# Routing tables of an attention and MoE kernel in 16 bits with columns innermost, and the first expert's low parts behind the slots' description

## The chip, the cores and the metric

The kernel runs on one core of one Trainium2 chip. Its time is the device time of one execution in microseconds (us); the median of three runs is 889.3 us (888.17 to 893.38).

## The reference

Three layers follow one another. Attention with a forget gate runs over 4 batches, 8 heads, 576 positions and a head dimension of 64: the scores get `cum[i] - cum[j]` of the logarithm of the gates added, then a causal mask, a softmax and the product with v. Its output is x, 2304 tokens of 512. A mixture of experts follows: each token goes to the one of 8 experts whose logit is greatest.

```python
e_idx = np.argmax(x @ w_gate, axis=1)
for e in range(E):
    mask = e_idx == e
    h = np.maximum(x[mask] @ w1[e], 0.0)
    out[mask] = gate_w[mask, None] * eom[mask, e, None] * (h @ w2[e])
```

Here w1[e] is 512 x 1024 and w2[e] is 1024 x 512. A dense layer of width 2048 with a rational activation ends it. All results are float32; TensorE's operands are kept as a high and a low part, with three products each.

## The kernel before

**Attention.** 16 pairs of heads are worked through, and a planner (class Plan) orders their instructions from costs and due times; it writes the order of all engines, which is then fixed. For each pair GpSimd (POOL) makes three arrays for each of the two heads: kl (L416), the low half of qs (L425) and q2s (L430). TensorE's scores (L456 and L457) need them. Between these POOL sends six DMAs (L873) that fill with zeros the part of y_d that only a spill would write. Small constant arrays are made by POOL at the start (L928 to L936): s1 with the slot numbers, row with the 128 places of a slot, tokv with the tokens' numbers.

**Routing.** Tokens are sorted by expert into slots of 128 rows. For the 20 columns of 128 tokens, VectorE (DVE) finds each token's position `pos` (L1003), its slot `sidx` (L1007) and its place in the slot `pp` (L1009). From these it builds one-hot arrays: `so` (column x slot, L1012), `rs` (`so` times the token's number, L1015) and `op_` (column x place, L1021, four instructions for five columns each, as float32 against float32 into float16). TensorE multiplies `op_` and `rs` for all 20 columns into `pid` (L1026), and DVE converts that to integers: `ids` (L1028), the token in each place of each slot. Meanwhile x is scaled, and SP stores it to x_d (L823), five stores for the last batch.

**Slots.** POOL gathers the rows of x of slot s from x_d with an indirect DMA by `ids` (gather, L1203); three are sent at once. TensorE runs 24 matmuls without use in between (warm, L1347), then transposes slot 0 (trans_x, L1222), ScalarE (ACT) and DVE split it into colAh (L1097) and colAl (L1088), and the products with the expert's weights follow: mm1 (two halves of w1, units 0 and 1) and mm2 (two halves of w2, units 2 and 3). Each of these is four matmuls of the high parts (L1228), four with the low part of the slot's rows (L1235), four with the low part of the weights (L1231). split_unit makes the high part of a unit on ACT (L1056) and the low part on DVE (L1058), two instructions of 128 x 1024 each. slot_info (L1162 to L1185) is 21 small DVE instructions on 25 partitions; they write esl, from which SP, ACT, DVE and PE read whether a slot begins a new expert, and SP sends the next expert's weights (L1136) into `raw` once both parts of the unit there are made. The weights of the dense layer are decoded between the slots; the first decode's load is d8 (L1283) and its first DVE instruction is L1287.

Once the routing begins, the order on each engine is that of the program:

```python
for s in range(3):
    gather(s)
warm(24)
split_unit(0, hi=False)
split_unit(1, hi=False)
trans_x(0, col_of(0))
slot_info()
```

Of the kernel before, what the change touches and what calls it, by code (L numbers as in the profile page):

```python
# [9 lines left out]
F32 = mybir.dt.float32  # L10
F32R = mybir.dt.float32r
BF16 = mybir.dt.bfloat16
F16 = mybir.dt.float16
# [124 lines left out]
def tile_attention_moe_mlp(  # L138
# [81 lines left out]
    with ExitStack() as actx, ExitStack() as rctx:  # L220
# [646 lines left out]
        for u in range(4):  # L867
            plan.op((NPAIR - 5 + u) * SPAN, {"SP": 2900}, lambda e, u=u: nc.sync.dma_start(out=raw[u], in_=w_src(u, 0)), [st[NPAIR - 7 + u]["o_ot"]])
        n = 0
        for s in range(NPIPE, NSLOT):  # L870
            for c in range(0, DM, 2 * P):
                n += 1
                plan.op((2 + n // 2) * SPAN, {"POOL": 1100}, lambda e, s=s, c=c: nc.gpsimd.dma_start(  # L873
                    out=y_d[s * P : (s + 1) * P, c : c + 2 * P].rearrange("p (a q) -> p a q", q=P),
                    in_=qs[0].bitcast(F32)[:, :, S:],
                ), [st[2 + n // 2]["o_ot"]])
# [11 lines left out]
        with tc.manual_schedule():  # L888
            plan.emit()

# [37 lines left out]
        s1 = iota([P, NSLOT], [[1, NSLOT]], 0, 0, "s1")  # L928
        nc.gpsimd.tensor_scalar_add(s1, s1, ROUND)

        row = iota([P, P], [[-1, P]], 0, 0, "row")
        nc.gpsimd.tensor_scalar(row, row, 1.0 / P, (P - 1) / (2.0 * P), op0=ALU.mult, op1=ALU.add)
        pcol = iota([P, 1], [[0, 1]], 0, 1, "pcol", const)

        tokv = iota([P, B, NI], [[S, B], [P, NI]], -(NT // 2), 1, "tokv").rearrange("p b i -> p (b i)")
# [64 lines left out]
        for i in (3, 0, 4, 2, 1):  # L1000
# [7 lines left out]
        pp = t_([P, NCOL], name="pp")  # L1008
        nc.vector.scalar_tensor_tensor(pp, sidx, ROUND, pos, ALU.subtract, ALU.subtract)  # L1009
        SS = [P, NCOL, NSLOT]  # L1010
        so, rs = t_(SS, F16, name="so"), t_(SS, F16, name="rs")
        nc.vector.tensor_tensor(  # L1012
            so, s1.unsqueeze(1).to_broadcast(SS), sidx.unsqueeze(2).to_broadcast(SS), ALU.is_equal
        )
        nc.vector.tensor_tensor(rs, so, tokv.unsqueeze(2).to_broadcast(SS), ALU.mult)  # L1015
        op_ = ptp.tile([P, 2, NI, S], F32, tag="pT", name="op_").rearrange("p h i s -> p (h i s)").bitcast(F16)
        op_ = op_[:, : NCOL * P].rearrange("p (c q) -> p c q", q=P)
        pid = ps_r("pid")
        for c0 in range(0, NCOL, NI):
            cs = slice(c0, c0 + NI)  # L1020
            nc.vector.tensor_tensor(  # L1021
                op_[:, cs], row.unsqueeze(1).to_broadcast([P, NI, P]),
                pp[:, cs].unsqueeze(2).to_broadcast([P, NI, P]), ALU.is_equal,
            )
            for c in range(c0, c0 + NI):
# [35 lines left out]
    for u in range(4):  # L1061
        split_unit(u, lo=False)
# [588 lines left out]
```

## Time and profile before

| | us |
|---|---|
| median of three runs | 889.3 |
| the profiled execution | 889.93 |
| its span, from the first to the last instruction | 888.2 |
| what lies around the span | 1.7 |
| attention and routing, up to the write of `ids` | 211.4 |
| slots and the dense layer, from there to the end | 676.8 |

Times in the rows further down are counted from the start of the span. A row of a timeline has the start, the length, the engine, the line, the operation, the tiles written and read, their shape and type, the count of instructions merged, and in brackets the idle time of the engine just before and what ended it.

### The profile page before, as it was taken

The page shows a single profiled execution, that of the slowest core. Times are in us where ns is not written, and L with a number is a line of the kernel's source. Part 1 is how long each engine was busy: PE and PEld are TensorE (multiplying, and loading weights), DVE is VectorE, ACT ScalarE, POOL GpSimd, SP SyncE. Part 2 cuts the span into 40 slices and gives each one's busy share as a digit, 9 for nine tenths or more (in the row PEclk, how much of TensorE's full clock was granted, in tenths as well). Part 3 has the DMA queues.
Part 4 walks back from the last instruction along what each step waited for, and adds up shares of the span by engine and source line. Part 5 has one row for each costly group of instructions (what it writes and reads, how often), then busy time and mean ns, then how long its engine had stood idle before and what let it go on. Part 6 is the DMA issues. An engine that isn't in the chain of part 4 may idle for free. (4 is left out here: it accounts for less than half of the span.)

```text
span 888.2 us, 15292 instructions
## 1 busy us (share of the span) xinstructions
PE 849.3 (96%) x4667; PEld 705.0 (79%) x4667; DVE 747.9 (84%) x1428; ACT 615.6 (69%) x1282; POOL 337.5 (38%) x364
## 2 busy tenths in 40 slices
PE   6999898996999999999999999999999999999997
PEld 6787786764888887888787788899888889988885
DVE  7798999778798878778876999898898878988882
ACT  4889897876465667567545878777676667777772
POOL 7888586502113232223241233343233224324222
PEclk9999999997999999999999999999999999999999
DMA  6776567604866588789564121010000001000001
GB/s 167 167 182 168 154 175 212 199 27 151 298 218 217 177 263 310 226 288 316 195 218 154 48 72 37 0 60 24 13 36 25 12 1 57 16 1 36 1 0 48
DMA packets 49130, 110.32 MB, mean 124 GB/s; under 512 B 8405, under 2 KB 12526, under 8 KB 49038
## 3 DMA queue, kind: packets, MB, share of 16 engines
q1 hardware_dynamic: 36910, 69.90, 26.4%
q0 software_dynamic: 12128, 39.34, 13.3%
q8 instruction: 40, 0.66, 0.3%
q14 instruction: 52, 0.43, 0.2%
HBM read 151.79 MB, written 20.35 MB: 194 GB/s over the span
## 5 line engine op out<-in xcount | busy, mean ns | idle before, releaser
L1519 POOL TENSOR_TENSOR gl<-raw,gh 128x512 fp32r<-128x512 f32 (+1 forms) x71 | 84.2, 1186 | 207.3 <-ACT gh L1517 127.2
L1535 PE MATMUL pa<-wu,gl 128*128 128x512 f32 x256 | 100.6, 393 | 1.1 <-POOL gl L1519 1.1
L1533 PE MATMUL pa<-wu,gh 128*128 128x512 f32 x256 | 101.2, 395 | 0.0
L1534 PE MATMUL pa<-wu,gh 128*128 128x512 f32 x256 | 100.1, 391 | 0.0
L1492 ACT ACTIVATE raw<-ph 128x512 f32<-128x512 f32 (+1 forms) x80 | 44.3, 554 | 78.1 <-PE ph L1484 74.8
L1058 DVE TENSOR_TENSOR wu<-raw,wu 128x1024 fp32r<-128x1024 f32 x64 | 75.2, 1219 | 8.0 <-ACT wu L1056 6.6
L511 ACT ACTIVATE pr<-t,mn 128x384 f32<-128x384 f32 (+3 forms) x128 | 70.7, 557 | 16.0 <-DVE mn L479 15.4
L1505 DVE SCALAR_TENSOR_TENSOR raw<-raw,coef,raw 128x512 f32<-128x512 f32 (+1 forms) x80 | 66.2, 827 | 17.8 <-ACT raw L1501 15.1
L1495 DVE SCALAR_TENSOR_TENSOR raw<-raw,babs 128x512 f32<-128x512 f32 (+1 forms) x80 | 58.3, 729 | 20.9 <-ACT raw L1493 20.2
L1482 PE MATMUL ph<-colAh,wi 128*128 128x512 f32 x192 | 74.9, 390 | 1.0 <-ACTq L1423 0.7
L1484 PE MATMUL ph<-colAh,wi 128*128 128x512 f32 x192 | 74.7, 389 | 0.0
L1483 PE MATMUL ph<-colAl,wi 128*128 128x512 f32 x192 | 74.7, 389 | 0.0
L1056 ACT ACTIVATE wu<-raw 128x1024 fp32r<-128x1024 f32 x64 | 63.8, 1066 | 4.1 <-DMA raw<-in_w_dram 2.2
L479 DVE CUSTOM_DVE_ANT_0 t<-s,mask 128x384 f32<-128x384 f32 (+3 forms) x128 | 57.8, 484 | 6.5 <-PE s L457 3.0
L1506 DVE SCALAR_TENSOR_TENSOR raw<-raw,cbias 128x512 f32<-128x512 f32 (+1 forms) x80 | 57.6, 720 | 2.3
L1500 ACT ACTIVATE raw<-raw,cbias 128x512 f32<-128x512 f32 (+1 forms) x80 | 55.0, 687 | 6.3 <-DVE raw L1495 5.8
L1494 ACT ACTIVATE raw<-ph,neg 128x512 f32<-128x512 f32 (+1 forms) x80 | 59.3, 741 | 0.0
L1535 PEld LDWEIGHTS pa<-wu,gl 128*128 128x128 f32 x256 | 48.0, 188 | 12.7 <-POOL gl L1519 2.4
L1497 DVE SCALAR_TENSOR_TENSOR raw<-raw,coef,ph 128x512 f32<-128x512 f32 (+1 forms) x80 | 55.5, 694 | 2.5
L1533 PEld LDWEIGHTS pa<-wu,gh 128*128 128x128 f32 x256 | 48.1, 188 | 9.5 <-ACT gh L1517 0.7
L1534 PEld LDWEIGHTS pa<-wu,gh 128*128 128x128 f32 x256 | 48.1, 188 | 9.0
L1507 DVE SCALAR_TENSOR_TENSOR raw<-raw,raw 128x512 f32<-128x512 f32 (+1 forms) x80 | 52.4, 655 | 2.4
(263 smaller groups left out, 2391.9 us busy)
## 6 DMA issues: line engine op xcount, KB each, us to landing
raw<-in_w_dram SPq DMA_DIRECT2D x92, 1024.0 KB
rk<-in_kT_dram SPq DMA_DIRECT2D x30, 288.0 KB
rq<-in_qT_dram SPq DMA_DIRECT2D x30, 288.0 KB
d<-in_w_in_dram POOLq DMA_DIRECT2D x16, 512.0 KB
d<-in_w_out_dram POOLq DMA_DIRECT2D x16, 512.0 KB
y_d<-ys SPq DMA_DIRECT2D x22, 256.0 KB
v<-in_v_dram SPq DMA_DIRECT2D x16, 256.0 KB
wo_d<-d POOLq DMA_DIRECT2D x16, 256.0 KB
```

The source lines that it names most:

```text
L511: nc.scalar.activation(u["pr"][:, sl], u["t"][:, sl], AF.Exp, bias=u["mn"][:, m : m + 1], scale=-1.0, accum_out=sm[:, i, 2 * hp + h : 2 * ...
L1056: nc.scalar.activation(w[:, 0], r, AF.Copy)
L1058: nc.vector.tensor_tensor(w[:, 1], r, w[:, 0].bitcast(F32), ALU.subtract)
L1482: nc.tensor.matmul(out_, wh, hi[:, :, c], start=(c == 0), stop=False)
L1483: nc.tensor.matmul(out_, wh, lo[:, :, c], start=False, stop=False)
L1484: nc.tensor.matmul(out_, wl_, hi[:, :, c], start=False, stop=(c == KD - 1))
L1494: nc.scalar.activation(u_, ph, AF.Identity, scale=neg[:, 3:4], bias=neg[:, 2:3])
L1505: nc.vector.scalar_tensor_tensor(u_, u_, coef[:, 0:1], rr, ALU.subtract, ALU.mult)
L1519: low.tensor_tensor(d["gl"], d["u_"], d["gh"].bitcast(F32), ALU.subtract)
L1533: nc.tensor.matmul(a_, gh[:, sl], wh, start=(m == 0), stop=False)
L1534: nc.tensor.matmul(a_, gh[:, sl], wl_, start=False, stop=False)
L1535: nc.tensor.matmul(a_, gl[:, sl], wh, start=False, stop=(m == MF - 1))
```

## The change

The one-hot arrays get their columns innermost (place x column and slot x column), in two halves of ten columns, and all their operands are float16. The constant arrays grow to that full shape: row is 128 x 10 and slot_n is 25 x 20 for each partition. They are made by POOL behind the zero fills of y_d, one piece behind each. The slot's number is brought to float16 by one more DVE instruction (sn). TensorE takes `op_` and `rs` with a step of ten and twenty elements.

```diff
+        NC2 = NCOL // 2
+        slot_n = wk.tile([P, NSLOT, NCOL], F16, name="slot_n", bufs=1)
+        row = wk.tile([P, P, NC2], F16, name="row", bufs=1)
...
+        tables = [
+            numbers(row[:, :P2], [[-1, P2], [0, NC2]]), numbers(row[:, P2:], [[-1, P2], [0, NC2]], -P2),
+            units(row[:, :P2]), units(row[:, P2:]),
+            numbers(slot_n, [[1, NSLOT], [0, NCOL]]), numbers(tokv, [[S, B], [P, NI]], -(NT // 2), 1),
+        ]
...
-        pp = t_([P, NCOL], name="pp")
+        pp, sn = t_([P, NCOL], F16, name="pp"), t_([P, NCOL], F16, name="sn")
...
+        nc.vector.tensor_scalar_add(sn, sidx, -ROUND)
+        SS, PC = [P, NSLOT, NCOL], [P, P, NC2]
...
+        def places(g):
+            nc.vector.tensor_tensor(
+                op_[:, g], row, pp[:, g * NC2 : (g + 1) * NC2].unsqueeze(1).to_broadcast(PC), ALU.is_equal
+            )
+
         pid = ps_r("pid")
...
+        places(0)
+        nc.vector.tensor_tensor(so, slot_n, sn.unsqueeze(1).to_broadcast(SS), ALU.is_equal)
+        nc.vector.tensor_tensor(rs, so, tokv.unsqueeze(1).to_broadcast(SS), ALU.mult)
+        for g in range(2):
+            if g:
+                places(1)
+            for c in range(NC2):
+                n = g * NC2 + c
+                nc.tensor.matmul(pid[:, :NSLOT], op_[:, g, :, c], rs[:, :, n], start=(n == 0), stop=(n == NCOL - 1))
...
-    for u in range(4):
+    for u in range(3):
         split_unit(u, lo=False)
...
-        warm(24)
+        warm(20)
+        slot_info()
         split_unit(0, hi=False)
+        trans_x(0, col_of(0))
         split_unit(1, hi=False)
-        trans_x(0, col_of(0))
-        slot_info()
...
-                split_unit(3, hi=False)
+                split_unit(3)
```

On DVE, from the slot's number to the first low part of x, the order before was this (info is the tile of slot_info; wu_3345 and wu_3346 are the weights of units 0 and 1):

```order
L1007 TENSOR_SCALAR sidx<-pos 128x20
L1009 SCALAR_TENSOR_TENSOR pp<-sidx,pos 128x20
L1012 TENSOR_TENSOR so<-s_3184,sidx 128x500
L1015 TENSOR_TENSOR rs<-so,tokv 128x500
L1021 TENSOR_TENSOR op__3306<-row,pp 128x640 x4
L1028 TENSOR_SCALAR ids<-pid 128x25
L1058 TENSOR_TENSOR wu_3345<-raw_82,wu_3345 128x1024 x2
L1058 TENSOR_TENSOR wu_3346<-raw_83,wu_3346 128x1024 x2
L1088 TENSOR_TENSOR colAl<-px,colAh 128x512
L1162 TENSOR_SCALAR info<-send_3203,pcol 25x9
```

Both low parts and colAl stood between `ids` and the first instruction of slot_info. Now the same stretch of DVE begins so:

```order
L1029 TENSOR_SCALAR sidx<-pos 128x20
L1031 SCALAR_TENSOR_TENSOR pp<-sidx,pos 128x20
L1032 TENSOR_SCALAR sn<-sidx 128x20
L1039 TENSOR_TENSOR op__3307<-row,pp 128x1280
L1045 TENSOR_TENSOR so<-slot_n,sn 128x500
L1046 TENSOR_TENSOR rs<-so,tokv 128x500
L1039 TENSOR_TENSOR op__3307<-row,pp 128x1280
L1054 TENSOR_SCALAR ids<-pid 128x25
L1188 TENSOR_SCALAR info<-send_3204,pcol 25x9
```

Two instructions of twice the length stand for the four, the first of them ahead of `so`, and slot_info comes right behind `ids`. Behind its last instruction (L1211) DVE goes on with the low parts; L1313 was L1287, and L1112 was L1086, the low part of slot 0's hidden rows:

```order
L1211 TENSOR_TENSOR esl<-info 25x1
L1084 TENSOR_TENSOR wu_3346<-raw_82,wu_3346 128x1024 x2
L1114 TENSOR_TENSOR colAl<-px,colAh 128x512
L1084 TENSOR_TENSOR wu_3347<-raw_83,wu_3347 128x1024 x2
L1114 TENSOR_TENSOR colAl<-px,colAh 128x512
L1146 TENSOR_LOAD esl
L1150 COMPARE_AND_BRANCH
```

The low part of unit 1 now stands behind colAl of slot 0. On POOL, in the attention, a pair of fills and the last array of a pair of heads stood so:

```order
L416 TENSOR_TENSOR kl_119<-rk,kh 64x576
L425 TENSOR_TENSOR qs_113<-rq,qs_113 64x576
L873 DMA y_d<-qs_113 128x2x128 x2
L430 TENSOR_SCALAR q2s_117<-rq 64x576
L416 TENSOR_TENSOR kl_120<-rk,kh 64x576
```

Now the tables come between them:

```order
L416 TENSOR_TENSOR kl_119<-rk,kh 64x576
L425 TENSOR_TENSOR qs_113<-rq,qs_113 64x576
L891 DMA y_d<-qs_113 128x2x128
L880 TENSOR_SCALAR row<-row 128x640
L891 DMA y_d<-qs_113 128x2x128
L875 IOTA slot_n 128x500
L430 TENSOR_SCALAR q2s_117<-rq 64x576
L416 TENSOR_TENSOR kl_120<-rk,kh 64x576
```

Ahead of this place one half of row was numbered behind the first fill, the other behind the second, and the first half got its units behind the third; so five of the six pieces stand ahead of this q2s.

## Rows read from the trace of the kernel before

**Rows 1.** The page: busy time of each engine, its share of the span, instructions.
```profile
PE 849.3 (96%) x4667; PEld 705.0 (79%) x4667; DVE 747.9 (84%) x1428; ACT 615.6 (69%) x1282; POOL 337.5 (38%) x364
```

**Rows 2.** What PE waited for, 195 to 888 us: total, times, longest.
```profile
PE pid L1026 <- DVE op__3306 L1021: 7.0, 4, 5.7
...
PE px L1222 <- DMA xg<-x_d,ids: 0.4, 1, 0.4
```

**Rows 3.** Timeline of DVE, 206 to 229 us.
```profile
206.36 0.18 DVE L1009 SCALAR_TENSOR_TENSOR pp<-sidx,pos 128x20 f32<-128x20 f32 x1
206.46 0.67 DVE L1012 TENSOR_TENSOR so<-s,sidx 128x500 f16<-128x500 f32 x1
207.17 0.68 DVE L1015 TENSOR_TENSOR rs<-so,tokv 128x500 f16<-128x500 f16 x1
207.76 3.02 DVE L1021 TENSOR_TENSOR op__3306<-row,pp 128x640 f16<-128x640 f32 x4
211.19 0.18 DVE L1028 TENSOR_SCALAR ids<-pid 128x25 int32<-128x25 f32 x1 [0.40 <-PE pid L1026]
211.49 4.63 DVE L1058 TENSOR_TENSOR wu<-raw,wu 128x1024 fp32r<-128x1024 f32 x4
...
218.22 0.21 DVE L1162 TENSOR_SCALAR info<-send,pcol 25x9 f32<-25x9 f32 x1
...
221.24 0.15 DVE L1185 TENSOR_TENSOR esl<-info 25x1 int32<-25x1 f32 x1
...
223.36 0.43 DVE L1287 TENSOR_SCALAR d<-d 128x512 uint32<-128x512 uint32 x1 [0.79 <-DMA d<-in_w_in_dram]
...
227.41 0.68 DVE L1086 SCALAR_TENSOR_TENSOR colAl<-px,colAh 128x512 fp32r<-128x512 f32 x1
```

**Rows 4.** Timeline of PE, 210 to 229 us.
```profile
210.84 0.31 PE L1026 MATMUL pid<-rs,op__3306 128*128 128x25 f16 x5 [0.43 <-DVE op__3306 L1021]
211.00 4.84 PE L1347 MATMUL ph<-identf 128*128 128x256 bf16 x24
216.25 0.63 PE L1222 MATMUL px<-identf,xg 128*128 128x128 f32 x4 [0.42 <-DMA xg<-x_d,ids]
...
228.71 1.08 PE L1235 MATMUL py<-wu,colAl 128*128 128x512 f32 x4
```

**Rows 5.** Timeline of POOL, 212 to 220 us.
```profile
212.23 1.47 POOL L1203 DMA_INDIRECT xg<-x_d,ids  x1 [19.50 <-DVE ids L1028]
214.00 1.83 POOL L1203 DMA_INDIRECT xg<-x_d,ids  x1 [0.30 <-issue]
216.14 0.95 POOL L1203 DMA_INDIRECT xg<-x_d,ids  x1 [0.30 <-issue]
...
218.34 1.16 POOL L1283 DMA_DIRECT2D d<-in_w_in_dram  x2
```

**Rows 6.** L1203's semaphore waits on POOL: length in ns, start in us.
```profile
L1203 POOLq EVENT_SEMAPHORE  x1: 5733/5733/5733, 204.4 to 204.4; - x1
...
L1203 POOLq EVENT_SEMAPHORE  x1: 974/974/974, 210.4 to 210.4; - x1
```

**Rows 7.** Stretches of 0.25 us: length, PE busy, granted clock, DMA share, GB/s.
```profile
204.75:205.00 0.25, 0.00 (x0) 0.99 0.00 0
...
215.00:215.25 0.25, 0.25 (x3) 0.53 0.77 311
```

**Rows 8.** Timeline of POOL, at the start and in the attention.
```profile
14.07 0.24 POOL L921 IOTA row<- 128x128 f32 x1
...
14.54 0.13 POOL L921 IOTA pcol<- 128x1 f32 x1
...
70.60 1.42 POOL L425 TENSOR_TENSOR qs<-rq,qs 64x576 fp32r<-64x576 f32 x1 [0.61 <-DVE mn L479]
...
73.55 0.67 POOL L430 TENSOR_SCALAR q2s<-rq 64x576 fp32r<-64x576 f32 x1
```

**Rows 9.** Timeline of PE: the scores that use that q2s.
```profile
78.07 0.33 PE L457 MATMUL s<-kl,q2s 128*128 128x384 f32 x1
```

More of the change, by code (lines that the diff above doesn't have):

```diff
@@ L868, in tile_attention_moe_mlp, with numbers, units, fill @@
             plan.op((NPAIR - 5 + u) * SPAN, {"SP": 2900}, lambda e, u=u: nc.sync.dma_start(out=raw[u], in_=w_src(u, 0)), [st[NPAIR - 7 + u]["o_ot"]])
+        NC2 = NCOL // 2
+        slot_n = wk.tile([P, NSLOT, NCOL], F16, name="slot_n", bufs=1)
+        row = wk.tile([P, P, NC2], F16, name="row", bufs=1)
+        tokv = wk.tile([P, NCOL], F16, name="tokv", bufs=1)
+        def numbers(t, pattern, base=0, per_row=0):
+            return lambda: nc.gpsimd.iota(
+                t, pattern=pattern, base=base, channel_multiplier=per_row, allow_small_or_imprecise_dtypes=True
+            )
+        def units(t):
+            return lambda: nc.gpsimd.tensor_scalar(t, t, 1.0 / P, (P - 1) / (2.0 * P), op0=ALU.mult, op1=ALU.add)
+        P2 = P // 2
+        tables = [
[3 more added lines that the diff above has]
+        ]
+        def fill(s, c):
+            def go(e):
+                nc.gpsimd.dma_start(
+                    out=y_d[s * P : (s + 1) * P, c : c + 2 * P].rearrange("p (a q) -> p a q", q=P),
+                    in_=qs[0].bitcast(F32)[:, :, S:],
+                )
+                if tables:
+                    tables.pop(0)()
+            return go
         n = 0
@@ L872, in tile_attention_moe_mlp @@
                 n += 1
[L873 to L876, printed above, removed]
+                plan.op((2 + n // 2) * SPAN, {"POOL": 1100}, fill(s, c), [st[2 + n // 2]["o_ot"]])
         wl = ec.tile([P, NHP, 32], F32, name="wl")
@@ L889, in tile_attention_moe_mlp @@
             plan.emit()
+        assert not tables
         choose, gates_a, gates_x, gates_b, rows_t, rows_m, rows_a, rows_d = last_of
@@ L1007, in tile_attention_moe_mlp @@
         nc.vector.tensor_scalar_add(sidx, pos, ROUND)
[L1008 removed]
+        pp, sn = t_([P, NCOL], F16, name="pp"), t_([P, NCOL], F16, name="sn")
         nc.vector.scalar_tensor_tensor(pp, sidx, ROUND, pos, ALU.subtract, ALU.subtract)
[L1010 removed]
+        nc.vector.tensor_scalar_add(sn, sidx, -ROUND)
+        SS, PC = [P, NSLOT, NCOL], [P, P, NC2]
         so, rs = t_(SS, F16, name="so"), t_(SS, F16, name="rs")
[L1012 to L1015, printed above, removed]
         op_ = ptp.tile([P, 2, NI, S], F32, tag="pT", name="op_").rearrange("p h i s -> p (h i s)").bitcast(F16)
[L1017 to L1026 removed]
+        op_ = op_[:, : NCOL * P].rearrange("p (g q c) -> p g q c", g=2, c=NC2)
+        def places(g):
+            nc.vector.tensor_tensor(
+                op_[:, g], row, pp[:, g * NC2 : (g + 1) * NC2].unsqueeze(1).to_broadcast(PC), ALU.is_equal
+            )
+        pid = ps_r("pid")
+        places(0)
[7 more added lines that the diff above has]
+                nc.tensor.matmul(pid[:, :NSLOT], op_[:, g, :, c], rs[:, :, n], start=(n == 0), stop=(n == NCOL - 1))
         ids = const.tile([P, NSLOT], I32, name="ids")
```

6 lines of the change are left out of this document (removed).

## The prediction

> **What bounds the kernel now.** I read the page first: PE is busy for 96% of the span, DVE for 84% [rows 1]. The kernel is a chain of PE work, so a change pays only where PE stands still. The list of what PE waited for, from the routing to the end, shows where: 7.0 us for `op_`, the one-hot places that DVE builds, 5.7 of them in one piece [rows 2]. That is the largest wait on the list. So whatever brings the first products of slot 0 forward moves the end by as much, unless PE runs into something else in the next slots.
>
> The timelines of DVE, PE and POOL around 205 to 217 us give the chain. DVE builds so, rs and op_ from 206.46 to 210.78 [rows 3]; PE ends `pid` at 211.15 [rows 4]; ids is written from 211.19 to 211.37 [rows 3]; POOL starts the first gather at 212.23 and is done with it after 1.47 us, at 213.70 [rows 5]; PE begins the transposes at 216.25, 2.55 us after that, and had waited for the gather's data [rows 4]. Between them PE runs the 24 warm matmuls.
>
> A second view decides what the first edit is worth: POOL's semaphore waits ahead of the gather [rows 6]. One began at 204.4 and lasted 5.73 us, to 210.13; it is for the stores of x. Only then came the wait for ids, from 210.4, 0.97 us long, to 211.40. So the gather can't start before the stores are in, however early ids is.
>
> **The change, step by step.** *The one-hots.* pp keeps its start, 206.36 [rows 3]. sn adds 0.10 us, the spacing of such small instructions (206.36 to 206.46), and the first `places`, which waits for pp, some 0.1 more: 206.57. Before, four op_ instructions of 640 elements took 3.02 us with 0.82 for the last, so one follows another after 0.73 us, 0.67 of it streaming and 0.07 around it: one element in 1.04 ns. No row has a two-operand instruction with all operands in 16 bits, so I bound it. At that same rate, 1280 elements take 1.40 each, and with so at 0.71 and rs at 0.59 behind it (their spacing before) the second places ends at 210.75; as fast again, places cost 0.73 each, so 0.45, rs 0.33, and the end comes at 208.90. The nearest row for the faster rate is L1287, one operand of 512 elements in 0.43 us [rows 3], against 0.82 for 640 with two: DVE does stream two elements in that time where its operands allow it. I take the faster one. The Trainium skill (VectorE: DVE Perf Modes, What auto-detection actually checks) says that an instruction with only 16-bit tensors of step one streams two elements a cycle; by that page the end is estimated at 208.9 too, and no row here shows it.
>
> PE then has ten matmuls left, not five: 0.31 us for five [rows 4], 0.47 for ten if the step of ten elements in the weights costs nothing; I bound that by 0.1 us for each of the ten, 1.0 in all. So ids is out at 209.65, or at 210.6 with slow weight loads, against 211.37 before. Its wait on POOL had 0.97 us; POOL's other wait ends at 210.4 anyway. The gather therefore starts 0.8 to 0.97 us earlier, at 211.26: of 1.72 us won on DVE, 0.75 are lost to the stores.
>
> *slot_info ahead of the low parts.* The first two gathers took 1.47 and 1.83 us beside the four L1058 instructions (211.49 to 216.12), the third 0.95 when those were over [rows 3, 5]. Now 21 small instructions on 25 partitions stand there, from 218.22 to 221.39 before, so 3.2 us. I take 0.97 for the first gather, 0.5 less; the bounds are 0 and 0.52. A rule speaks against this: the Trainium skill (SBUF — State Buffer, Who interferes with whom) holds that a DVE instruction with two SBUF inputs disturbs GpSimd's reads but not its writing, and so not the making of descriptors. The three rows say otherwise here; by the rule the gather keeps its 1.47 us and its data come 0.97 earlier, not 1.47.
>
> With 2.55 us from the gather's end to the transposes, these start at 214.78 instead of 216.25: 1.47 us won. The low parts are hidden: slot_info ends at about 212.9, unit 0's low part 2.3 us later (4.63 for four), at 215.2, and PE wants it behind the transposes and eight matmuls of slot 0, of which four take 1.08 [rows 4], so not before 217; unit 1's follows colAl and is there at 219.1, wanted sixteen matmuls later, past 221. If that cover were gone, each would cost up to 2.3 us. Unit 3's high part, moved on ACT into slot 0, is wanted by slot 0's second mm2, sixty matmuls behind the first, and costs nothing.
>
> *What is late next.* DVE's L1287 waits for d8 until 223.36, and behind it come unit 2's low part and, at 227.41 to 228.10, the colAl that PE takes at 228.71 [rows 3, 4]. That leaves 0.6 us of room. With PE 1.47 us ahead, d8 has to land 0.86 earlier. POOL sends it behind the gathers (218.34 before, [rows 5]), so 1.44 earlier; but SP now sends the next expert's weights as soon as unit 0's low part is done, and that megabyte shares the DMA engines with d8, where before it came behind it. Between 0.6 (d8 no earlier) and 1.47 won, I take 1.1.
>
> *The tables on POOL.* Iota took 0.24 us for 128 elements and 0.13 for one, so 0.87 ns for an element; q2s, two operations on 576 elements, took 0.67 [rows 8]. By these, two iotas of 640 cost 0.69 each, two units 0.72 each, slot_n 0.56: 3.4 us ahead of the q2s at 73.55, less the 0.61 of idle time at 70.60 [rows 8]. That q2s then ends at 77.0, not 74.22, and PE uses it at 78.07 [rows 9]. It is hidden by 1 us. The six small instructions that leave the start stood before idle time: nothing.
>
> *The clock.* It fell to half during PE's longest wait (0.99 at 204.75) and rose in the quarter from 215.00, 4.2 us into the warm matmuls of 211.00 [rows 4, 7]. Twenty matmuls at half clock last 4.27 us (256 columns at 1.2 GHz each). They run from 209.43 to 213.7, and PE then idles for 1.1 us, not 0.4. I take the same rise as before, at the end of the run, and nothing for it; the other end is a rival.
>
> **Sum.** 889.93 for the profiled execution less 1.1 is 888.8. That execution lies 0.63 above the median of the runs shown, so for a median: 888.2 us.
>
> **Rivals.** *The clock comes late, or falls again in the longer gap.* For it: it fell in a wait, and rose only 1 us before the transposes [rows 4, 7]. Against it: that wait was 5.7 us long, the gaps now are near 1 us. Slot 0's products then run at half clock for as long as the rise took before, 4.2 us, and lose half of it, 2.1: 889.3 - 1.1 + 2.1 = 890.3.
>
> *POOL's tables hold the scores (the slower side).* The place is the q2s of 73.55; it decides from 4.4 us of tables on (1 us more than above). For it: no row shows an iota or a two-step operation in 16 bits on POOL. Against it: the rows for 32 bits leave 1 us. At twice the price, 6.8 us, q2s ends at 80.4 and PE is held 2.3 us: 889.3 + 2.3 - 1.1 = 890.5.
>
> *One element at a time.* ids is then at 211.5 and the gather gains only its shorter length less 0.1: 888.9.
>
> *The gather is as long as before*, by the rule above: 0.9 won, 888.4.
>
> *d8 is no earlier, or later:* 0 to 0.6 won, 888.7 to 889.3. For it: 0.79 us of waiting already there [rows 3].
>
> **How the numbers follow.** Forecast 0.42, clock 0.23, tables 0.10, one element 0.07, long gather 0.08, d8 0.10. The likeliest case reaches from 887.8 to 888.7 by itself; single runs of the kernel before lie from 888.17 to 893.38, so a median of three may stand 2 us off. The range is 886.0 to 891.8: below, the full 1.47 us from the lowest run (886.7) and some unknown; above, the dear rivals and as much again as the gain. A measurement of this kernel can tell about 1% (8.9 us) from no change; no case comes near that: faster 0.02, same 0.95, slower 0.03.
>
> **What would show it.** Right: places at 0.8 us each, ids near 209.7, POOL's wait for the stores as the last before the gather, a first gather of 0.95 to 1.0 us, the transposes at 214.8, the clock up before the first products. Wrong: places at 1.4 us; a gather of 1.4; PE waiting near 78 for q2s, or in slot 0's first mm2 for colAl; half clock beyond 216.

## The result, and the profile after

The changed kernel takes 896.12 us (median of 11 runs) against 891.29 us (11 runs) of the kernel before on the same chip: ratio 1.0068, 95% interval [1.0042, 1.0094], so 6.1 us slower (3.7 to 8.4). Forecast were 888.2 us, range 886.0 to 891.8. The median lies outside, on the slower side. Of the 7.9 us between forecast and result 2.0 lie in the kernel before, whose median was 889.3 in the three runs shown ahead and is 891.29 here. The change's own execution that was profiled took 897.11 us with a span of 895.4; all times below are from its start.

The routing did what was forecast. VectorE's timeline, in the changed kernel (its lines are 22 to 26 higher: L1009 is now L1031, L1058 is L1084, L1287 is L1313):

```profile
212.00 0.18 DVE L1031 SCALAR_TENSOR_TENSOR pp<-sidx,pos 128x20 f16<-128x20 f32 x1
212.10 0.17 DVE L1032 TENSOR_SCALAR sn<-sidx 128x20 f16<-128x20 f32 x1
212.22 0.82 DVE L1039 TENSOR_TENSOR op__3307<-row,pp 128x1280 f16<-128x1280 f16 x1
212.96 0.41 DVE L1045 TENSOR_TENSOR so<-slot_n,sn 128x500 f16<-128x500 f16 x1
213.40 0.42 DVE L1046 TENSOR_TENSOR rs<-so,tokv 128x500 f16<-128x500 f16 x1
213.74 0.82 DVE L1039 TENSOR_TENSOR op__3307<-row,pp 128x1280 f16<-128x1280 f16 x1
215.42 0.18 DVE L1054 TENSOR_SCALAR ids<-pid 128x25 int32<-128x25 f32 x1 [0.86 <-PE pid L1052]
...
218.91 2.36 DVE L1084 TENSOR_TENSOR wu<-raw,wu 128x1024 fp32r<-128x1024 f32 x2 [0.15 <-issue]
...
228.89 0.43 DVE L1313 TENSOR_SCALAR d<-d 128x512 uint32<-128x512 uint32 x1 [0.31 <-DMA d<-in_w_in_dram]
```

Against [rows 3]: 1280 elements now take as long as 640 did, and from pp to ids 3.42 us pass (212.00 to 215.42) where 4.83 did (206.36 to 211.19). But pp itself comes at 212.00, not 206.36: 5.64 us are lost before the routing begins.

TensorE's timeline, to hold beside [rows 4]:

```profile
213.88 1.50 PE L1052 MATMUL pid<-rs,op__3307 128*128 128x25 f16 x20 [3.89 <-DVE rs L1046]
215.22 4.32 PE L1373 MATMUL ph<-identf 128*128 128x256 bf16 x20
220.42 0.63 PE L1248 MATMUL px<-identf,xg 128*128 128x128 f32 x4 [0.89 <-DMA xg<-x_d,ids]
222.06 1.55 PE L1254 MATMUL ph<-wu,colAh 128*128 128x512 f32 x4 [1.01 <-ACT colAh L1123]
223.41 1.91 PE L1261 MATMUL ph<-wu,colAl 128*128 128x512 f32 x4
225.12 1.55 PE L1257 MATMUL ph<-wu,colAh 128*128 128x512 f32 x4
226.50 0.60 PE L1248 MATMUL px<-identf,xg 128*128 128x128 f32 x4
```

The wait for the one-hots is 3.89 us where the longest was 5.7 [rows 2]. The transposes begin 8.42 us behind pp; before it was 9.89 (206.36 to 216.25). That is the 1.47 us that were forecast. Between the transposes and the first products 1.64 us pass, where the kernel before took 1.38 (216.25 to 217.63): 0.26 are lost there. Then three groups of slot 0's products go at half speed, the second wholly and the other two in part (1.91 us for its four matmuls, 1.08 at the full clock [rows 4]): from them to the next transposes 4.44 us pass, where the other kernel took 2.87 (217.63 to 220.50), so 1.57 are given back. The granted clock there (length, PE busy, clock, DMA share, GB/s), to hold beside [rows 7]:

```profile
219.25:219.50 0.25, 0.25 (x2) 0.93 0.88 360
...
222.50:222.75 0.25, 0.25 (x3) 0.89 0.92 336
222.75:223.00 0.25, 0.25 (x3) 0.50 0.73 180
...
226.00:226.25 0.25, 0.25 (x2) 0.78 1.08 434
```

It rose at the end of the warm matmuls, fell again at 222.7, after TensorE had idled 0.89 us before the transposes and 1.01 before the products, and rose at 226.

GpSimd's gathers, beside [rows 5]:

```profile
216.81 1.08 POOL L1229 DMA_INDIRECT xg<-x_d,ids  x1 [18.46 <-ACT wu L1082]
218.20 0.98 POOL L1229 DMA_INDIRECT xg<-x_d,ids  x1 [0.30 <-issue]
219.48 1.48 POOL L1229 DMA_INDIRECT xg<-x_d,ids  x1 [0.30 <-issue]
```

So the account of the profile is: 5.64 lost before the routing, 1.47 won in it, 0.26 lost behind the transposes, 1.57 lost by the clock, and 1.2 more lost between 226 and 496 us; together 7.2 us of span (888.2 to 895.4).

Where the 5.64 come from shows in attention. GpSimd's timeline there, to hold beside [rows 8]:

```profile
56.23 2.17 POOL L875 IOTA row<- 128x640 f16 x1
...
67.15 2.15 POOL L875 IOTA row<- 128x640 f16 x1
69.26 0.73 POOL L891 DMA_DIRECT2D y_d<-qs  x1
70.08 0.71 POOL L880 TENSOR_SCALAR row<-row 128x640 f16<-128x640 f16 x1
...
79.72 0.70 POOL L875 IOTA slot_n<- 128x500 f16 x1
80.51 0.67 POOL L430 TENSOR_SCALAR q2s<-rq 64x576 fp32r<-64x576 f32 x1
```

The iotas of row take 2.16 us each, not 0.69. The five tables that the forecast's 3.4 us counted come to 6.5, and all six to 6.7 (2.17, 2.15, 0.71, 0.76, 0.70 and 0.21). The same stretch on VectorE, and then what TensorE waited for from 53 to 100 us:

```profile
54.19 4.89 DVE L411 CAST kh<-rk 128x576 fp32r<-128x576 f32 x2
...
67.33 2.28 DVE L411 CAST kh<-rk 128x576 fp32r<-128x576 f32 x1
```

```profile
PE pt L598 <- DVE pT L293: 2.4, 1, 2.4
PE pt L598 <- ACT pT L291: 0.9, 1, 0.9
```

In the kernel before, VectorE's first place looked so, and a later one so:

```profile
53.74 1.78 DVE L411 CAST kh<-rk 128x576 fp32r<-128x576 f32 x2
...
151.18 2.26 DVE L411 CAST kh<-rk 128x576 fp32r<-128x576 f32 x1
```

Such a cast has a median of 0.45 us there. But nine of the 32 took 0.69 to 2.26, and each of these had begun while GpSimd was at an instruction; the first one above took 1.41 beside a qs that ended at 54.83. So GpSimd holds VectorE's casts without an iota too. In the changed kernel the first cast of the pair ends at 58.72 us and the one of 67.33 at 69.61, each 0.3 us behind the end of an iota (58.40 and 69.30). VectorE keeps its order, and the copy of pT behind the pair is what TensorE waits for at 57 to 60 us. Before, TensorE's waits over the same work, from 52 to 95 us, were 0.4 us in all.

By the times of the kernel before, TensorE is 3.1 us behind it at 57 us, 4.6 at 66, 4.0 from 77 to 95, 4.9 at 100 and 5.5 at 166 us. Of this 0.5 was there at 30 us, ahead of the first table, and what was lost behind 100 us was lost behind the last one, so 4.4 us of the profile lie where the tables stand.

### The profile page after: what moved, and what is told of

Read it like the earlier page. It is cut to its first block, busy times and chain, and to the rows that moved or that the text cites. A ratio compares the mean times of both kernels' runs of the same rounds, so it can differ in the third digit from the quotient of the medians.

```text
span 895.4 us, 15282 instructions
## 1 busy us (share of the span) xinstructions
PE 855.2 (96%) x4663; PEld 709.4 (79%) x4663; DVE 749.2 (84%) x1427; ACT 615.6 (69%) x1282; POOL 342.3 (38%) x365
## 5 line engine op out<-in xcount | busy, mean ns | idle before, releaser
L1084 DVE TENSOR_TENSOR wu<-raw,wu 128x1024 fp32r<-128x1024 f32 x64 | 75.3, 1219 | 8.0 <-ACT wu L1082 6.3
L598 PE MATMUL pt<-identf,pr 128*128 128x128 f32 x320 | 49.8, 284 | 7.7 <-ACT pr L511 4.2
```

What stands on the lines that cost most here:

```text
L1084: nc.vector.tensor_tensor(w[:, 1], r, w[:, 0].bitcast(F32), ALU.subtract)
```

## The experiments

Ratios are to the kernel before, run on the same chip beside each; a ratio of 0.001 is 0.9 us. Three theories: A, the tables hold attention (6 us); B, the clock in slot 0; C, the new order behind the gathers costs rather than wins.

**The tables alone (e1).** In the kernel before, the fills of y_d also build the tables, in arrays that nothing reads:

```diff
+ tables = [numbers(row_x[:, :P2], ...), ..., numbers(tokv_x, ...)]
- plan.op((2 + n // 2) * SPAN, {"POOL": 1100}, lambda e, ...: nc.gpsimd.dma_start(...), ...)
+ plan.op((2 + n // 2) * SPAN, {"POOL": 1100}, fill(s, c), ...)
```

> The kernel before, with nothing of the change but its tables: the six GpSimd instructions (four on row, one for slot_n, one for tokv) stand behind the same fills of y_d as in the changed kernel, in arrays that nothing reads; routing and the order behind it are those of before. Theory A (the tables hold the qs and q2s of attention's pairs, and with them the scores): routing's pp starts 5.2 to 6.0 us later than before's 206.4, the first 3 us of it at the pair that waits behind the first iota near 56 us, and the time is 5 to 6 us (0.6%) above before's. Rival (attention is longer in the changed kernel for another reason, the places of tiles or the waits that the planner set): pp starts within 1 us of 206.4 and the time stands at before's.

Ratio 1.0075 [1.0041, 1.0110], 6.7 us: as much as the whole change. TensorE waits 2.44 us for pT and 0.90 us for pT again, as in the changed kernel, and loses 4.5 us from 30 to 100 us, where that lost 4.4. pp starts at 214.1 us, 7.7 late where 5.2 to 6.0 were expected, but in an execution that was already 1.3 us late at 30 us and lost some 1.7 more at half clock from 108 to 111 us. Theory A holds.

**The tables late (e2, e3).** The changed kernel with the tables taken out of the fills and put behind the memset of sc for the last batch, where GpSimd has 13.7 us with nothing to do; e3 with `warm(24)` besides.

```diff
-                if tables:
-                    tables.pop(0)()
...
+        plan.op((NPAIR - 0.9) * SPAN, {"POOL": 6700}, build, [st[NPAIR - 2]["o_ot"]])
```

```diff
-        warm(20)
+        warm(24)
```

> The changed kernel, with its six table instructions taken from behind the fills and put behind the memset of sc for the last batch (near 177 us in before's trace), where GpSimd has 13.7 us with nothing to do; all else as changed. [...] Rival: pp stays near 212 and the time 5 to 6 us above before's. A third way: the tables beside VectorE's work on the last pair slow that down, and pp starts 1 to 3 us late.

> As the run with the tables late, with 24 warm matmuls as before the change instead of 20, so that TensorE works up to about where the first gathered rows arrive. Theory B (with 20 the engine is idle for 0.9 us behind them and slot 0's first products go at the lower clock, 1.6 us): first transposes no later than with 20, three groups of mm1(0) at 1.1 to 1.2 us each, time 1 to 1.6 us under the run with 20. Rival (the clock rises at its own time, with 20 as with 24): the two agree within 0.5 us and slot 0's products are as slow, or as fast, in both.

Ratios 1.0025 [1.0003, 1.0047] and 1.0031 [1.0009, 1.0054]. At 166 us, with no table yet, e2 is 1.6 us behind before's first profile and e3 0.2 ahead; then both lose 2.3 us up to 182 us. GpSimd's tables, then VectorE, in e2:

```profile
178.63 4.25 POOL L875 IOTA row<- 128x640 f16 x2
```

```profile
179.38 1.44 DVE L699 TENSOR_SCALAR sums<-sums 128x16 f32<-128x16 f32 x1
180.88 0.25 DVE L700 RECIPROCAL rc<-sums 128x16 f32<-128x16 f32 x1
181.05 1.85 DVE L699 TENSOR_SCALAR sums<-sums 64x8 f32<-64x8 f32 x1
182.94 0.20 DVE L700 RECIPROCAL rc<-sums 64x8 f32<-64x8 f32 x1
```

L699 takes 0.10 to 0.17 us where GpSimd runs nothing beside it; beside kl or q2s it took 0.4 to 1.2 in the kernel before too. Here the first ends with the first iota (178.63 + 2.1) and the second with the second (182.88), while the reciprocal between them runs beside the iota in its usual 0.25. GpSimd had nothing queued behind the tables, so this is no matter of its queue: the third way of the expectation came true, and VectorE's TENSOR_SCALAR stands while an iota runs. Theory B fails as a systematic cost: e2 with 20 warm matmuls and a gap of 1.13 us ran slot 0's first group in 1.19 us, at the full clock, and e3 is no faster. Over all profiles the half clock came four times where a gap stood before the transposes (gaps of 0.89, 0.94, 2.05 and 3.55 us) and stayed away with gaps of 0.96, 1.03 and 1.13. What decides it is not shown.

**The tables behind rc (e5, e6).** A small GpSimd instruction that reads rc goes ahead of the tables, so that they start behind the last L699. The planner put it later than I had expected, behind the last rc of the last batch; the tables ran from 196.4 to 203.0 us.

```diff
...
+            nc.gpsimd.tensor_scalar(scr[:TL], bt[B - 1]["rc"][:TL, NQ, 0:1], 1.0, 0.0, op0=ALU.mult, op1=ALU.add)
+            while tables:
+                tables.pop(0)()
...
```

e6 is the whole change with that; e5 (like e4, whose tables stood where e2 has them) has the one-hots with the order of before: `warm(24)`, both low parts ahead of slot_info, four high parts ahead of the routing.

```diff
-    for u in range(3):
+    for u in range(4):
         split_unit(u, lo=False)
...
-        warm(20)
-        slot_info()
+        warm(24)
         split_unit(0, hi=False)
-        trans_x(0, col_of(0))
         split_unit(1, hi=False)
+        trans_x(0, col_of(0))
+        slot_info()
```

> Tables late, the one-hot arrays as changed, but the order behind the gathers as before the change (24 warm matmuls, both low parts ahead of slot_info, all four high parts ahead of routing). By the step of the prediction on the gather: ids 1.4 us earlier than before in relation to pp; the gather beside the low parts takes 1.4 to 1.5 us; transposes 0.8 to 1.0 us earlier than before (9.9 us behind pp), time 0.5 to 1 us under before's. Rival (the reorder is what wins): transposes at 9.5 to 9.9 us behind pp and the time at before's. Other rival (the one-hots win all 1.5 us): transposes at 8.4 us behind pp.

> As the run of the one-hots only, with one thing moved: the six table instructions stand behind a small GpSimd instruction that reads rc, so that they start after VectorE's last TENSOR_SCALAR on sums (L699) of the last batch, near 178.5 us, and end near 185.5 us, ahead of VectorE's next TENSOR_SCALAR (near 189.7 us). Theory A2 (an iota on GpSimd holds VectorE's TENSOR_SCALAR and casts from SBUF to SBUF until it ends, and with them what stands behind in VectorE's order; GpSimd's own queue is not what costs in the late place): L699 takes 0.15 us each again, the 2.3 us lost between 166 and 182 us in the run with the one-hots only are gone, pp starts within 0.5 us of before's place, and the time is 2 to 2.5 us under that run's, 0.5 to 1.5 us under before's. Rival (any GpSimd work there slows whatever VectorE does): 1.5 to 2.5 us lost again, at L729, L733 and the scores' copies, and no gain. Second rival (the lateness there comes from elsewhere, the memory the tables take or the planner's order): 2.3 us lost again with L699 at 0.15 us.

> The whole change as it stands (20 warm matmuls, slot_info first, low parts behind it), with the tables behind rc. Against the run with the order of before and the tables behind rc it tells what the reordering is worth where the tables cost nothing. Theory C (the reordering wins nothing at the gather, where the first one took 1.08 us beside the low parts too, and makes d's transfer land later, so that colAl of mm2(0,0) is late): transposes 8.1 to 8.5 us behind pp in both, mm2's low parts 1 to 2 us later here than there in relation to the transposes, time 1 to 2 us above that run's. Rival (as predicted: slot_info first shortens the gather by 0.5 us and hides the low parts): time 0.5 us under that run's.

e4: 1.0015 [0.9993, 1.0037], with the 2.3 us lost as in e2. e5: 0.9994 [0.9977, 1.0012]. e6: 1.0020 [1.0004, 1.0037]. In e5 the tables cost nothing: from the last reciprocal of rc to pp 11.50 us pass (196.02 to 207.52), and 11.48 in the kernel before (194.88 to 206.36), though the same 6.6 us of GpSimd's work run in between. VectorE has only TENSOR_TENSOR, TENSOR_REDUCE and a scan beside the iotas there. So the whole change less the price of its tables is 1.8 us slower than before (0.4 to 3.3), and the one-hots alone stand at before's time.

The transposes begin 8.47 and 8.63 us behind pp in e4 and e5, 8.28 in e6: the one-hots won 1.3 to 1.4 of the 1.47 us by themselves. In e4 the first gather took 1.08 us although the low parts ran beside it. Behind the transposes TensorE waits 1.0 us for colAh in every profile with the new order, and 0.7 in every one with the old. Counted from pp, the first products begin at 9.8 to 10.0 us in e4, e5 and e14, and at 9.7 to 10.3 in the profiles with the one-hots and the new order whose gather no transfer of d delays: there the new order has won nothing.

**The order alone (e7), and what it costs (e9, e10, e13, e14).** e7 is the kernel before with the reordering only (and `split_unit(3)` whole in slot 0).

```diff
-        split_unit(0, hi=False)
-        split_unit(1, hi=False)
-        trans_x(0, col_of(0))
-        slot_info()
+        slot_info()
+        split_unit(0, hi=False)
+        trans_x(0, col_of(0))
+        split_unit(1, hi=False)
```

> The kernel before with the reordering alone (slot_info, then the low parts of unit 0, the transposes, those of unit 1; unit 3 split whole in slot 0; 24 warm matmuls; one-hots and tables as before). Theory C: transposes at 9.4 to 9.9 us behind pp as before (9.9), d lands 1 to 2.5 us later, low parts of mm2(0,0) 0.5 to 2 us later in relation to the transposes, time 0 to 2 us above before's. Rival (prediction's step on slot_info): the first gather 0.97 instead of 1.47 us, transposes 0.5 us earlier, time 0.5 us under before's.

1.0023 [1.0003, 1.0042]. The gain that I had expected of it is there: first gather 1.11 us instead of 1.47, transposes 9.34 us behind pp instead of 9.89. It is lost right behind. VectorE, then TensorE's wait, in e7:

```profile
226.25 0.43 DVE L1287 TENSOR_SCALAR d<-d 128x512 uint32<-128x512 uint32 x1 [3.17 <-DMA d<-in_w_in_dram]
...
230.30 0.68 DVE L1086 SCALAR_TENSOR_TENSOR colAl<-px,colAh 128x512 fp32r<-128x512 f32 x1
```

```profile
PE py L1235 <- DVE colAl L1086: 1.7, 1, 1.7
```

With slot_info first, SyncE issues the first refill of raw at 217.87 us (221.97 before), a megabyte, ahead of d's two transfers, and the second one at 221.21. d lands at 226.25 instead of 223.36, in an execution whose routing was 0.8 us late, and VectorE stands before it with colAl behind. To take only this away, d's transfers were moved: ahead of all gathers (e9 with the new order, e10 with the old one), or behind the first gather (e13 new, e14 old), all four with the tables behind rc. The edit of e13 and e14; in e9 and e10 the same loop stands ahead of the gathers:

```diff
         for s in range(3):
             gather(s)
+            if s == 0:
+                for _ in range(2):
+                    held.append(True)
+                    doing.append(todo.popleft())
+                    next(doing[-1])
```

> The whole change (its order, 20 warm matmuls) with the tables behind rc, and one thing more: the first two transfers of d (1 MB) are issued on GpSimd ahead of the gathers instead of behind the fourth. Theory C2 (what the reordering costs is a collision: with slot_info first, SyncE issues the first refill of raw at 219.4 us, before or beside d's two transfers, the DMA engines are full from there on, d lands at 227.8 instead of 223.4, and VectorE, which keeps its order, stands 2.9 us before d's first piece and so brings colAl of mm2(0,0) late): no wait on d above 0.3 us, no wait of TensorE for colAl at mm2(0,0), time 1 to 2.5 us under the 894.1 (ratio 1.002) of the run without d first. Rival (the late low parts, not d, cost it): colAl is late by 1 to 2 us still. Second rival: d's megabyte beside the x_d stores moves the gathers' floor by 1 to 2 us, and the gain is given back there.

> The one-hots with the order of before and the tables behind rc, and d's first two transfers ahead of the gathers. d waited there only 0.58 us (VectorE idle), so theory C2 expects 0 to 1 us under the run without (ratio 0.9994 then, 0.998 to 0.9994 now): with d out of the way, the refills of raw meet a freer DMA, and the transfers that the pipeline waits for at 338 to 361 us (1.5 us each time) land up to 1 us earlier. Rival: the stream of weights lands by its own pace, same time within 0.5 us.

> The whole change (its order, 20 warm matmuls), tables behind rc, and d's first two transfers issued on GpSimd behind the first gather instead of behind the fourth: after the x_d stores, so that these are left alone, and some 4 us ahead of the first refill of raw. Theory C2 (the collision of d with the refills is what the new order costs): VectorE waits for d under 0.5 us, no wait of TensorE for colAl at mm2(0,0), time 1 to 2 us under that of the same kernel with d behind the fourth gather (ratio 1.002), so 0.999 to 1.001. Theory C3 (the low parts that come 4 us later move the refills, and these the stream that is waited for near 340 us): colAl on time, and yet the wait for raw near 340 us as long as it was (1.3 us or more) or longer, ratio 1.001 to 1.003.

> The one-hots with the order of before, tables behind rc, and d's first two transfers behind the first gather. Second and third gathers start 1.1 us later, which the pipeline does not feel (rows of slot 1 are wanted 4 us behind those of slot 0). Theory: d lands by 219 us, VectorE's wait for d (0.58 us) goes, all else as in the run without; ratio 0.998 to 1.000. Rival: d's transfers slow the first gather's rows, the transposes come 0.5 to 1 us later, ratio 1.000 to 1.002.

e9: 1.0044 [1.0026, 1.0061], e10: 1.0042 [1.0023, 1.0062]. The wait for d goes, but the second rival came true: the megabyte stands beside the stores of x, and in e10 the gather starts 2.7 us behind ids (208.63 to 211.35; 1.1 us in e5) and TensorE waits for its rows and loses the clock too:

```profile
215.65 0.63 PE L1259 MATMUL px<-identf,xg 128*128 128x128 f32 x4 [3.55 <-DMA xg<-x_d,ids]
217.01 1.85 PE L1265 MATMUL ph<-wu,colAh 128*128 128x512 f32 x4 [0.73 <-ACT colAh L1134]
```

e13: 0.9999 [0.9980, 1.0018], 1.9 us under e6, with d in time and no wait for colAl:

```profile
223.04 0.43 DVE L1324 TENSOR_SCALAR d<-d 128x512 uint32<-128x512 uint32 x1 [0.30 <-DVEq L1161]
```

So d beside the refills is where the new order loses its time in the profiles. The times alone do not carry this: the 1.9 us between e6 and e13, each against the kernel before on a chip of its own, are uncertain by some 2.2, and e14, which moves d in the old order, stands 2.0 us above e5: 1.0016 [0.9991, 1.0041].

**The prices of iotas (e8), and a second look at the kernel before (e11).** e8 is the kernel before with five iotas behind rc.

```diff
...
+            num(as_(64, 10), [[1, 64], [0, 10]])
+            num(as_(10, 64), [[0, 10], [-1, 64]])
+            num(as_(25, 20), [[-1, 25], [0, 20]])
+            num(as_(32, 20), [[-1, 32], [0, 20]])
+            num(one, [[-1, 640]])
...
```

> The kernel before, with five iotas into an array that nothing reads, behind the same small instruction on rc, to price the form by itself: [[1,64],[0,10]], [[0,10],[-1,64]], [[-1,25],[0,20]], [[-1,32],[0,20]] and [[-1,640]], all in 16 bits. If the price goes by the number of short inner runs (34 ns a run of 10 in the changed kernel, 28 ns a run of 20): 2.2, 0.4 to 0.7, 0.7, 0.9 and 0.3 to 0.7 us. If it goes by the sign of the step or by each number written (3.4 ns): 2.2 us for all of 640, and 0.7 us for the 500 only where the step is positive. Beside them VectorE has no TENSOR_SCALAR from SBUF to SBUF; by theory A2 the time stands at before's, within 0.5 us.

> The kernel before itself, once more, for a second profile of it: how far two executions of one kernel differ at the places where the others were read. If the waits for raw at 338 us (1.5 to 2.8 us in the changed ones, none in before's first profile) are the kernel's own, this one too shows pp near 206.4 and no wait at 338 us. If they are chance (how the transfers meet), it shows one of 0.5 to 2 us there, and TensorE at 342 us is 0.5 to 2 us behind the first profile.

GpSimd in e8, the first, third, fourth and fifth:

```profile
194.36 2.15 POOL L889 IOTA one<- 128x640 f16 x1
...
197.36 0.67 POOL L889 IOTA one<- 128x500 f16 x1
...
198.09 0.81 POOL L889 IOTA one<- 128x640 f16 x1
...
198.97 0.66 POOL L889 IOTA one<- 128x640 f16 x1
```

The second took 0.7. Neither the sign of the step nor the count of numbers sets the price, the runs do: 640 numbers in runs of 10 take 2.15 us, in runs of 20, 64 or 640 they take 0.81, 0.7 and 0.66. The short runs are also more (64, against 32, 10 and 1), and what is length and what is number is not told apart here; in e17 further down, 16 runs of ten take 0.62. The one time of e8 was 890.56 us, before's median 892.34: no loss to be seen in one run.

e11 shows how far two executions of one kernel differ: pp at 205.42, and at 342 us TensorE is 0.75 us behind the first profile although it was 0.95 ahead at the routing. Between them lies a wait for a unit's weights, on ScalarE, first in e11 and then in e14:

```profile
338.29 2.01 ACT L1056 ACTIVATE wu<-raw 128x1024 fp32r<-128x1024 f32 x2 [1.89 <-DMA raw<-in_w_dram]
```

```profile
339.55 2.01 ACT L1093 ACTIVATE wu<-raw 128x1024 fp32r<-128x1024 f32 x2 [3.33 <-DMA raw<-in_w_dram]
```

In e14 TensorE was 1.5 us ahead at the second transposes and 2.0 us behind at 342 us.

**The refills earlier (e15, e16).** slot_info in three pieces: four instructions between the last one-hot and ids, ten between the low parts and the first colAl, the rest (with esl's last column in a tile of its own) where it stood; e16 with d behind the first gather as well. The edit is shown against e5:

```diff
+        nc.vector.tensor_scalar(eq[q], send0[q], pcol[q], None, op0=ALU.is_equal)
...
         nc.vector.tensor_scalar_add(ids, pid[:, :NSLOT], float(NT // 2))
...
+        slot_info()
         trans_x(0, col_of(0))
-        slot_info()
+        slot_info2()
```

> The one-hots with the order of before, tables behind rc, and slot_info taken apart: four of its instructions between the last one-hot and ids, where VectorE waits 0.9 us for TensorE, twelve between the low parts and the first colAl, where it waits 1.3 us, and the rest (the column that says how full a slot is) where it stood. SyncE's first two refills of raw can be issued near 217 us instead of 221.8. If the start of the refills sets the stream (theory C3): the wait for raw near 340 us gets 1 us or more shorter, ratio 0.997 to 0.999. If the collision with d rules (theory C2): d lands 2 to 3 us later, colAl of mm2(0,0) 1 to 2 us late, ratio 1.001 to 1.003.

> Both: slot_info taken apart and d's first two transfers behind the first gather. By theory C2 and C3 alike the best of all: d lands before the refills start, the refills start 4 us earlier, ratio 0.996 to 0.999. If neither helps (the stream near 340 us goes by its own pace, set by the slots' own rhythm behind slot 0): ratio 0.999 to 1.001, with a wait for raw near 340 us as before.

1.0007 [0.9985, 1.0029] and 1.0000 [0.9976, 1.0024]. The first refill went out at 216.67 and 218.38 us, 11.4 us behind pp (15.6 before). e15 ran into the collision once more (3.70 us of waiting for d, mm2(0,0) 2.14 us late for colAl); e16 did not, and still waited 1.66 us for raw at 339.4. Both lost time at the start as well: the first gather took 2.1 us, and the transposes began 9.62 us behind pp, 1.0 later than in e5. So earlier refills did not take away the wait near 340 us; what they would give with a gather as short as e5's is not shown.

**How the iotas cost (e12, e17).** e12 writes row's two iotas with the repeats outermost, through a rearranged view; e17 leaves them as they are, in four instructions each.

```diff
-            numbers(row[:, :P2], [[-1, P2], [0, NC2]]), ...
+            numbers(row[:, :P2].rearrange("p q c -> p c q"), [[0, NC2], [-1, P2]]),
...
```

```diff
...
+                for q in range(q0, q0 + P2, P2 // 4):
+                    numbers(row[:, q : q + P2 // 4], [[-1, P2 // 4], [0, NC2]], -q)()
...
```

> The changed kernel with everything in its place, and only the two iotas of row written with the ten repeats outermost (inner run of 64 numbers, written with a stride of ten) instead of innermost. By the prices measured by themselves (2.15 us with runs of 10, 0.75 us with runs of 64) the tables go from 6.7 to 3.9 us if the strided writing costs nothing. Theory A: an iota of 0.75 us holds VectorE's cast and GpSimd's queue by that much less, twice; pp starts 2.5 to 4 us earlier than in the changed kernel and the time is 2.5 to 4 us under its 896.1 (ratio 1.002 to 1.004 to before). Rival (what costs is that anything more stands in GpSimd's queue there, whatever its length): same time as the changed kernel. If the strided writing costs as much as the short runs, the iotas take 2 us again and nothing changes, which tells nothing of the rest.

> The changed kernel with everything in its place, and only the two iotas of row written as four instructions each, of 16 runs of ten, one behind the other (0.55 to 0.6 us each by 2.15 / 4, so 2.2 to 2.4 us together). GpSimd's queue is held as long as in the changed kernel; VectorE's cast, which stood 2.3 us and more beside an iota (0.46 us by itself), can begin when the first of the four ends. Theory A2 (the hold of VectorE is what costs in attention too): casts of 0.5 to 1.1 us beside the iotas, TensorE 1.5 us or less late at 57 us (3.1 in the changed kernel) and 3 us or less at 66 us (4.5), time 1.5 to 3 us under the changed kernel's (ratio 1.0035 to 1.005). Theory A1 (GpSimd's queue: kl and q2s behind the iotas are late): 3 us at 57 us and 4.5 us at 66 us as there, ratio 1.0065 or more. If VectorE is held through all four, it cannot be told apart, and the time stays too.

e12 missed its aim: writing with a stride of ten made each iota dearer, 3.01 us (55.43 to 58.44). It is useful as a larger dose: 1.0099 [1.0066, 1.0131], TensorE 6.6 us behind at 66 us (4.6 in the changed kernel), with waits of 3.3 and 1.7 us where that had 2.4 and 0.9. But 1.2 of the 6.6 us come from half clock, from 61 to 64 us, behind the first of these waits.

e17: 1.0048 [1.0024, 1.0071]. The iotas took 2.48 and 2.43 us together. GpSimd's first four of them, and VectorE's casts at the first and the second place:

```profile
56.34 2.48 POOL L875 IOTA row<- 128x160 f16 x4
```

```profile
54.29 4.17 DVE L411 CAST kh<-rk 128x576 fp32r<-128x576 f32 x2
...
66.91 0.45 DVE L411 CAST kh<-rk 128x576 fp32r<-128x576 f32 x1
```

It had been expected that a cast could begin behind the first of the four. That did not come: the second of the pair began at 55.63 us, ahead of all four, and ended at 58.47, 0.3 us behind the third. The one of 66.91 took its usual time, but it had begun 0.1 us ahead of its iotas (67.01). Still, at the first place TensorE loses as much more as the pair of casts is longer: the pair took 4.17 us in e17, 4.89 in the changed kernel and 5.73 in e12 (1.78 before), and from 30 to 57 us TensorE lost 1.9, 2.7 and 3.5. So the hold of VectorE is what costs first.

From 30 to 66 us TensorE lost 2.2 us in e17 instead of 4.1. But by 100 us it had lost 4.5, as much as in the changed kernel, with new waits for sums (0.51) and pr (1.10). Under the hold another limit may lie, GpSimd's queue: between 55 and 92 us it had 2.3 us of idle time before the change (0.61 [rows 8], and 1.73 ahead of a kl at 84), and 6.7 us of tables went in. The 4.4 by this subtraction stand beside the 4.4 that the changed kernel lost up to 100 us; for e17 it gives 4.9 beside 4.5, for e12 6.1 beside 6.9, of which 1.2 are the half clock. That the queue sets the whole loss is argued from this, not shown. In the whole time e17 and the changed kernel can't be told apart.

No version is shown to beat the kernel before. e5, e13 and e16 stand at its time, 6 us under the changed kernel.

## Why the prediction was wrong, point by point

- *The one-hots*: right. Twice the rate, 0.82 us for a places; the last one ends 2.56 us behind pp, 2.54 were worked out. The ten matmuls with strided weights ended 0.82 us behind the last places, where 0.47 to 1.47 were the bounds and the low end was taken: 0.35 too cheap.
- *The floor of the gather*: right. It started 4.81 us behind pp, 4.90 forecast. It does not bind always: in e2, e3 and e12 the gather came 4.5 to 4.6 us behind pp, as far behind ids as in the kernel before, so ids came last there. e9 and e10 confirm the floor from the other side: what slows the stores of x delays the gather.
- *slot_info ahead*: the transposes came 8.42 us behind pp, exactly as forecast, but not by the steps as put. With the one-hots alone (e4) the gather was 1.08 us beside the low parts. Alone in the kernel before (e7), the reordering does shorten it, by 0.36, and brings the transposes 0.5 us forward; on top of the one-hots it is worth about 0.25 (8.0 to 8.6 us from pp with it, 8.5 to 8.6 without). Gathers beside the low parts took from 1.08 to 2.13 us over the runs, those beside slot_info or nothing from 0.94 to 1.11. So the rule that the prediction quotes from the Trainium skill (SBUF — State Buffer, Who interferes with whom), by which the low parts leave the making of descriptors alone, fits some of these gathers, and most are lengthened against it. At the first products the 0.25 are gone again, by the longer wait for colAh.
- *What is late next*: a step that failed. I had seen that the next expert's weights now share the DMA engines with d8, and bounded the result by 0.6 won. It was a loss: 1.4 to 1.7 us of waiting for colAl in e6 and e7. In time the order costs 2.1 us by e7 (0.3 to 3.7). My bound took "d8 no earlier" as the worst; counted from pp it came 0.9 us later in e6 and 2.1 in e7. In the changed kernel's own profile, whose first products went at half clock, d came 16.89 us behind pp (17.00 before), and TensorE did not wait for colAl.
- *The tables on POOL*: the step that decided. The price was taken per element from an iota without repeats (0.69 us; it measured 2.16), so that the sum came to 3.4 and not 6.5 us. Above all, the cover was read at one place, the q2s at 73.55. The loss came at the first iota, 17 us earlier, where VectorE's cast was held, and TensorE did not wait for that q2s at all. The prediction has no term for a VectorE instruction that GpSimd holds, though the kernel before shows a cast held for 1.41 us in that very place. The rival was named, with a chance of 0.10 and a decision point of 4.4 us of tables that was passed; its price of 2.3 us was too small, because it counted one wait of TensorE for one q2s: TensorE lost 4.4 us from 30 to 100 us, and the tables alone cost 6.7 us of time (3.7 to 9.8) in e1.
- *The clock*: not forecast in the likeliest case; in the profile it cost 1.57 us, against 2.1 in the rival. By e2 and e3 it is not a price of `warm(20)`; what decides it in an execution stays open.
- *"The end moves as much as the first products"*: not borne out, and not refuted by the times. Of 1.3 us won by e5 the time shows 0.5 (-1.1 to 2.0). Near 340 us most profiles, before's second one among them, wait 0.8 to 3.3 us for raw (four do not: before's first, the changed kernel's, e4 and e12), and what was ahead is level again. That this wait swallows the gain is argued from the profiles, and what sets its place was not found: earlier refills (e15, e16) did not move it. The last 1.2 us of the profile's account are of the size by which two executions of the kernel before differ there (1.7 us between 208 and 342 us).

## What to carry to other kernels

Before work is put on an engine that looks half idle, subtract the idle time of its queue in just that stretch from all that is added, and look on the other engine that reads and writes the same memory for instructions that it would hold; being off the critical path is cover for neither. Price an instruction by its access pattern, not by its elements, or measure it alone where nothing waits. When a step is moved forward, list the transfers that it releases and what they will now run beside: here the gain of an earlier step came back as a later transfer.

## What was not expected of the hardware

An iota of 640 numbers in runs of ten costs 2.15 us, in runs of 20 or more 0.66 to 0.81; with runs of 64 that were written at a stride of ten it cost 3.01. VectorE's casts and TENSOR_SCALARs from SBUF to SBUF that come behind an iota on GpSimd stand until it ends (0.10 to 0.46 us became 1.4 to 2.8), and a cast was not let in between three iotas in a row (e17); kl, qs and q2s on GpSimd hold them too (up to 2.26). RECIPROCAL, TENSOR_TENSOR, reductions and copies out of PSUM beside an iota took their usual time. At half clock, matmuls whose 128 by 128 weights lie at a step of ten elements, and their moving operand at one of twenty, followed each other after 0.06 us, where with both side by side it was 0.03; which of the two steps costs is not shown.
